# A new order for the 610 steps of the first part of an attention, MLP and mixer kernel

## The chip, the cores and the metric

The kernel runs on one core of a Trainium2 chip. The metric is the device time of one execution in microseconds (us), as the median of the runs. A program's five engines that matter here are TensorE (PE in the profile, with PEld for its weight loads), VectorE (DVE), ScalarE (ACT), GpSimd (POOL) and SyncE (SP, which issues nearly all DMAs).

## What is computed

Three layers in a row, cut to their cores. The first is an attention of 2 batches, 8 heads, 768 positions and head size 64 over a local window and 24 block summaries; the second a layer norm with an MLP of width 2048; the third a mixer over tokens and channels.

```python
# attention
k_sum = k.reshape(B, H, nb, block, D).max(axis=3)
v_sum = v.reshape(B, H, nb, block, D).mean(axis=3)
scores = concat([where(abs(i - j) < 16, scale * q @ k.T, -1e9), scale * q @ k_sum.T + log(block)])
a = softmax(scores);  x = a @ concat([v, v_sum])
# MLP
x = x + relu(layer_norm(x) * g @ w_ch1) @ w_ch2
# mixer
theta = x @ w_theta
u = x + w_tok_r @ (x * cos(theta)) + w_tok_i @ (x * sin(theta))
out = u + relu(u @ w_ch)
```

## The kernel before

The 1536 rows (2 batches of 768) are 12 tiles of 128 rows; tile t has two units, 2t and 2t+1, of four heads each. The MLP works on three chunks of four tiles and goes over 16 slices of its width. The first part of the program, up to the middle of the second chunk, is written as a string of words, `START`. Each word is one step: letters for the kind, a number for the tile, unit, chunk row or weight block. `run` reads the string and issues each step's instructions when its word comes. Every engine runs its instructions in the order in which they were issued, so the string sets the order on each engine, and nothing reorders it afterwards. The words of the steps are:

- DMA loads, issued on SP: `k` keys (0 to 3 of batch 0, 4 to 7 of batch 1), `q` queries (q0 and q1 on ACT's queue), `v` values, `b` values for the block means, `l` a weight block, `M` masks, `J` identity, `G` the norm's gain; `F` with a number not divisible by 3 copies the block means' rows from one value buffer to another.
- attention: `K` block maxima of the keys (DVE), `u` block sums (POOL), `Z` turns them (PE), `F0`, `F3` copy them (ACT); `S` scores of a tile (PE), `m` row maxima (DVE), `N` and `e` bias and exponentials of a unit (ACT), `T` its transposes (PE), `p` or `d` their copy out of PSUM (DVE or ACT), `V` times the values (PE), `R` and `o` the division (DVE).
- layer norm: `n`, `s`, `c` (DVE), `P` (POOL), `dg` (ACT), `fl` (PE), `fh` (ACT), `fz` (DVE) for chunk 0; `h`, `y`, `t` (ACT, DVE, DMA) for chunk 1.
- weights: `A` (ACT), `D` (DVE), `H` (ACT) or `HV` (DVE), `I` (POOL) or `IV` (DVE) turn block l into two float16 halves.
- MLP: `U` up (PE), `i` (ACT), `j` (DVE), `X` down (PE), `Y` adds a result to its tile (DVE).

Buffers are rings that hand out what was given back first: 8 PSUM banks (an `S` takes two, a `T`, `V`, `fl`, `U` one each; `e`, `p` or `d`, `o`, `fz`, `j` give them back), 3 query buffers (q3 overwrites q0's after S0), 3 value buffers, 4 raw buffers for `b` and `l`, 3 buffers for exponentials. The first 12 units' `T` and `V` and the first 8 units' `S` have a dummy matmul (`fill`, from the tile `idle`) ahead of them, and 16 more stand at the very start. Only the words' order is touched by the change; `SECOND` and all later parts, whose order a planner (`Plan`) makes, stay.

Of the kernel before, what the change touches and what calls it, by code (L numbers as in the profile page):

```python
# [14 lines left out]
U16 = mybir.dt.uint16  # L15
# [16 lines left out]
CH = 3 * P  # L32
MC = 4 * P
START = """
q1 J0 q0 M0 k3 k0 k1 k2 b0 b3 b2 b1 q2 v0 v1 v2 K3 K0 K1 K2 G0 S0 u2 k7 k5 S1 m0 k4 k6 m1 N0 u3 e0 l3 S2 m2 q4 N1 e1 q3
m3 N2 u0 b4 e2 T1 m4 q5 T0 m5 d1 T2 N4 p0 e4 u1 b7 p2 N5 T4 N3 e3 e5 T3 b6 K7 Z0 T5 F0 K5 V0 F2 K4 F1 V1 d3 R0 o0 K6 d4
v3 R1 o1 A3 n0 S4 D3 HV3 b5 IV3 S3 q7 m8 m9 N8 e8 s0 c0 S5 u7 q6 N9 m6 e9 m7 V4 N7 m10 q8 e7 V3 m11 u6 l0 N6 R4 V2 o4
N10 d5 R3 o3 T8 N11 R2 v4 o2 V5 n1 e6 u5 T7 l7 s1 c1 v5 d8 T6 d7 R5 o5 T9 d6 n2 V7 e10 s2 u4 l2 V6 R7 e11 o7 T10 R6 v6
o6 S7 n3 d10 P0 l6 s3 A0 d9 Z1 D0 P3 V8 dg0 m15 l1 F3 V9 P1 q10 R8 o8 fl0 HV0 P2 T11 F4 dg1 IV0 v7 fh0 S6 R9 o9 d11 c2
N15 fz0 dg2 fl1 q9 m12 e15 V10 c3 fl2 R10 T15 dg3 o10 m14 V11 fh1 p15 fh2 fl3 F5 fz1 N12 v8 fh3 R11 S8 o11 e12 fz2 fz3  # L40
A2 T12 m13 q11 A6 U0 D2 N13 e13 D6 l5 H2 p12 l10 H6 m16 T13 i0 V12 IV2 I6 N16 V15 e16 j0 U1 R12 o12 N14 R15 e14 o15 p13
A1 m17 V13 n5 i1 T16 D1 N17 v9 e17 T14 S9 R13 l8 o13 H1 s5 j1 A5 I1 p14 T17 A7 m19 V14 P5 D5 N19 e19 D7 l4 H5 X0 R14
l13 o14 H7 I5 m18 v10 A10 IV7 N18 e18 D10 X1 A8 p17 l14 HV10 D8 I10 HV8 A4 T18 l12 p16 I8 V17 d18 D4 V16 V18 A13 R17
l21 o17 T19 H4 R16 v11 o16 R18 d19 I4 S10 o18 D13 HV13 l9 U2 n4 I13 A14 m21 m20 N21 e21 D14 U3 i2 s4 l20 HV14 N20 c4
I14 e20 j2 A21 n7 P4 U4 i3 s7 D21 A12 P7 j3 l23 H21 D12 h4 I21 X2 i4 HV12 l15 c7 A9 I12 j4 h7 D9 U5 A20 HV9 l11 D20 I9
HV20 A23 l18 y7 U6 I20 i5 D23 t7 A15 j5 l17 H23 D15 U7 I23 y4 l22 A11 HV15 t4 c5 I15 T21 D11 A18 V19 p21 X3 l16 D18
HV18 l19 R19 I18 o19 HV11 X4 n9 i6 I11 h5 s9 c9 P9 j6 A17 V21 y5 i7 T20 R21 X5 t5 o21 d20 j7 A22 D17 D22 H17 l27 X6
HV22 l28 n6 I22 h9 s6 c6 I17 X7 y9 A16 P6 n8 D16 A19 V20 HV16 l30 s8 S11 I16 D19 R20 H19 l26 o20 U8 n10 I19 m22 h6 m23
P8 N22 e22 s10 c10 U9 P10 i8 y6 N23 e23 j8 t6 c8 A28 U10 i9 D28 A30 j9 l29 H28 D30 A27 T23 IV28 U11 l24 d23 D27 i10
HV30 H27 l31 j10 A26 IV30 X8 D26 h10 IV27 H26 l25 y10 A29 X9 IV26 i11 D29 j11 H29 A24 T22 IV29 V23 d22 D24 X10 A31 R23  # L50
o23 H24 D31 A25 IV24 H31 X11 D25 IV31 H25 IV25 U12 U13 i12 j12 U14 i13 j13 U15 i14 j14 X12 t10 t9 X13 i15 j15 X14 h8
X15 y8 t8 U16 Y3 Y1 Y0 Y2 U17 i16 j16 X16 i17 j17 X17 U18 U19 i18 j18 X18 i19 j19 X19 U20 U21 i20 j20 X20 i21 j21 U22
X21 i22 j22 X22 V22 U23 R22 o22 n11
"""
SECOND = """
s11 c11 P11 U24 i23 h11 j23 y11 X23 t11 i24 j24 X24 U25 U26 i25 j25 X25 i26 U27 j26 X26 i27 U28 j27 U29 i28 j28 X27 i29
# [1093 lines left out]
```

## Time and profile before

| what | before |
|---|---|
| median of 3 runs | 479.9 us (479.78 to 479.94) |
| the profiled execution: its time | 483.72 us |
| its span, first to last instruction | 481.9 us |
| PE busy | 466.6 us (97%) |
| DVE, ACT, POOL busy | 310.5, 223.0, 229.9 us |
| mean granted PE clock | 0.992 |

A busy PE counts a matmul from its start to a modelled end, and neighbours overlap; a wait that is shorter than that overlap does not show as idle. What a step takes on PE is therefore read from the distance between the starts of two steps, and the number of instructions in a stretch from the counts in brackets.

### The profile page before, as it was taken

The numbers are of one execution on the slowest core, as the hardware profiler recorded it, in microseconds if no ns is written. First come the engines' busy times: TensorE is split into PE (matmuls) and PEld (weight loads), VectorE is DVE, ScalarE is ACT, GpSimd is POOL, SyncE is SP. The second block draws the span as 40 slices with busy tenths as digits, with TensorE's granted clock in tenths as the row PEclk, the third lists the DMA queues.
The fourth block names the chain that finished last, engine by engine and source line by source line (L and its number), as shares of the span: only waits on it lengthen the run. The fifth ranks groups of instructions, "written<-read, shape, count | busy, mean of one in ns | idle before, by whom it ended". The sixth has DMA issues, their size and how long they took to land. (4 is left out here: it accounts for less than half of the span.)

```text
span 481.9 us, 8629 instructions
## 1 busy us (share of the span) xinstructions
PE 466.6 (97%) x3360; PEld 245.9 (51%) x3360; DVE 310.5 (64%) x480; ACT 223.0 (46%) x469; POOL 229.9 (48%) x254
## 2 busy tenths in 40 slices
PE   8888999999999999999999999999998999999997
PEld 3556765445444444444444444444454554566664
DVE  4485899999961311258199898667749588942332
ACT  1564897744851110167176677545525246511122
POOL 3735115655300000049087868556698954792200
PEclk9997999999999999999999999999999999999999
DMA  8996858795681200067287853100076100010012
GB/s 285 307 315 205 264 180 259 253 226 192 203 251 29 43 0 0 1 172 200 65 224 224 238 177 95 39 1 1 0 186 196 23 0 18 33 51 18 0 50 98
DMA packets 44105, 61.71 MB, mean 128 GB/s; under 512 B 23478, under 2 KB 30528, under 8 KB 43680
## 3 DMA queue, kind: packets, MB, share of 16 engines
q1 hardware_dynamic: 43776, 60.63, 43.3%
q8 instruction: 26, 0.43, 0.4%
q10 hardware_dynamic: 288, 0.52, 0.4%
q14 instruction: 15, 0.12, 0.1%
HBM read 48.81 MB, written 6.68 MB: 115 GB/s over the span
## 5 line engine op out<-in xcount | busy, mean ns | idle before, releaser
L111 PEld LDWEIGHTS <-pc 128*128 128x128 f16 x996 | 96.8, 98 | 83.0 <-DMA tok_t<-spilled_t 2.5
L111 PE MATMUL ps<-pc,h 128*128 128x512 f16 x300 | 67.8, 379 | 0.0
L111 PE MATMUL ps<-xt,pc 128*128 128x512 f16 x288 | 65.3, 379 | 0.0
L108 PE MATMUL ps<-xt,pc 128*128 128x512 f16 x288 | 64.2, 379 | 0.0
L108 PE MATMUL ps<-pc,h 128*128 128x512 f16 x276 | 61.4, 379 | 0.0
L111 PE MATMUL ps<-tok_t,pc 128*128 128x384 f16 x288 | 48.8, 326 | 1.7 <-DMA tok_t<-spilled_t 1.7
L111 PEld LDWEIGHTS <-h 128*128 128x128 f16 x300 | 29.3, 98 | 35.4
L108 POOL TENSOR_TENSOR pc<-w,pc 128x512 f16<-128x512 f32 x20 | 27.1, 1361 | 37.6 <-ACT pc L108 22.4
L108 PEld LDWEIGHTS <-pc 128*128 128x128 f16 x288 | 27.8, 98 | 32.8
L108 PEld LDWEIGHTS <-h 128*128 128x128 f16 x276 | 26.8, 98 | 31.8
L108 DVE SCALAR_TENSOR_TENSOR h<-ps,h 128x512 f16<-128x512 f32 x23 | 15.8, 687 | 38.6 <-ACT h L108 38.4
L108 ACT ACTIVATE h<-ps 128x512 f16<-128x512 f32 x23 | 13.8, 600 | 53.8 <-PE ps L108 53.7
L111 PE MATMUL ps<-tok_b,pc 128*128 128x384 f16 x216 | 37.2, 326 | 0.1
L111 POOL TENSOR_TENSOR ve<-mv,eps 128x1 f32<-128x1 f32 x1 | 0.2, 193 | 77.6 <-DVE mv L111 77.6
L111 PE MATMUL ps<-x,pc 128*128 128x384 f16 (+1 forms) x204 | 32.2, 317 | 1.2 <-DVE x L111 1.2
L111 PE MATMUL ps<-th,x 128*128 128x512 f16 x144 | 33.0, 379 | 0.0
L111 DVE SCALAR_TENSOR_TENSOR h<-ps,h 128x512 f16<-128x512 f32 x25 | 17.1, 684 | 21.1 <-ACT h L111 21.1
L111 POOL TENSOR_TENSOR pc<-tr,pc 128x512 f16<-128x512 f32 (+1 forms) x18 | 19.0, 1060 | 20.7 <-ACT pc L111 20.7
L108 ACT ACTIVATE pr<-ps,nb 128x120 f32<-128x120 f32 x96 | 26.6, 365 | 3.9 <-PE ps L108 3.3
L108 POOL TENSOR_TENSOR raw<-raw 128x384 f32<-128x384 f32 (+3 forms) x32 | 18.6, 580 | 17.5 <-DMA raw<-in_vt 15.6
L111 DVE SCALAR_TENSOR_TENSOR w<-raw,hd 128x384 int32<-128x384 int32 (+1 forms) x23 | 22.5, 991 | 6.7 <-ACT hd L111 2.7
L108 DVE SCALAR_TENSOR_TENSOR w<-raw,hd 128x512 int32<-128x512 int32 x32 | 25.2, 795 | 1.1 <-ACT hd L108 1.0
(133 smaller groups left out, 785.9 us busy)
## 6 DMA issues: line engine op xcount, KB each, us to landing
raw<-in_w SPq DMA_DIRECT2D x32, 511.8 KB, 4.6
vw<-in_vp SPq DMA_DIRECT2D x12, 396.0 KB, 6.2
raw<-in_wtr SPq DMA_DIRECT2D x12, 383.8 KB, 4.1
raw<-in_wti SPq DMA_DIRECT2D x12, 383.8 KB, 3.8
k<-in_kw SPq DMA_DIRECT2D x8, 400.0 KB, 8.4
raw<-in_vt SPq DMA_DIRECT2D x8, 384.0 KB, 7.9
qt<-in_qd SPq DMA_DIRECT2D x10, 256.0 KB, 5.3
tok_t<-spilled_t SPq DMA_DIRECT2D x2, 1152.0 KB, 5.8
```

The source lines that it names most:

```text
L108: return getattr(getattr(self.nc, name), method)(*args, **kwargs)
L111: op = Op(len(self.ops), self.ENGINES[name], lambda: getattr(getattr(self.nc, name), method)(*args, **kwargs))
```

## The change

The string `START` holds the same 610 words in another order; no word is added or taken away, and nothing else in the kernel changes. On every engine the same instructions run, in other places. Two pairs of lines of the table:

```diff
-q1 J0 q0 M0 k3 k0 k1 k2 b0 b3 b2 b1 q2 v0 v1 v2 K3 K0 K1 K2 G0 S0 u2 k7 k5 S1 m0 k4 k6 m1 N0 u3 e0 l3 S2 m2 q4 N1 e1 q3
...
+q0 M0 k0 K0 k1 b2 k3 K1 k2 b1 K3 q2 K2 S0 S2 m1 u2 m0 b0 q1 N1 m5 u1 u0 b3 e1 S1 J0 m2 v2 N0 m4 e0 T0 T1 N5 e5 d1 m3
...
```

PE's steps up to the first `U` were

S0 S1 S2 T1 T0 T2 T4 T3 Z0 T5 V0 V1 S4 S3 S5 V4 V3 V2 T8 V5 T7 T6 T9 V7 V6 T10 S7 Z1 V8 V9 fl0 T11 S6 fl1 V10 fl2 T15 V11 fl3 S8 T12 U0

and are now

S0 S2 S1 T0 T1 T5 S3 Z0 T2 T4 V1 V0 S5 V5 T3 T6 V2 V3 V4 S4 T10 T7 V6 T11 S6 S8 V7 T8 T9 S7 V10 T13 fl1 V11 fl2 T12 V8 S9 fl0 V9 Z1 T17 T15 T16 V13 fl3 V12 S10 U0

On SP, the first loads of the program; k0 is the key tile of batch 0 and k1 that of batch 1, raw0 to raw3 hold block values (in_vt) or weights (in_w1, in_w2), qt0 to qt2 queries, vw0 to vw2 values. Before:

```order
L108 DMA ident_181<-in_ident 128x128
L108 DMA mask_l_179<-in_mask_l 69x384
L108 DMA mask_r_180<-in_mask_r 69x480
L108 DMA k0_185<-in_kw 128x800 x4
L108 DMA raw0_160<-in_vt 128x768
...
L108 DMA qt2_184<-in_qd 128x512
L108 DMA vw0_190<-in_vp 96x1056
...
L108 DMA g_sb_74<-in_g_ln 128x512
L108 DMA k1_186<-in_kw 128x800 x4
L108 DMA raw2_162<-in_w2 128x2047
L108 DMA qt1_183<-in_qd 128x512
```

And now:

```order
L108 DMA k0_185<-in_kw 128x800 x2
L108 DMA raw0_160<-in_vt 128x768
L108 DMA k0_185<-in_kw 128x800 x2
L108 DMA raw1_161<-in_vt 128x768
L108 DMA qt2_184<-in_qd 128x512
...
L108 DMA vw2_192<-in_vp 96x1056
L108 DMA qt0_182<-in_qd 128x512
L108 DMA vw0_190<-in_vp 96x1056
...
L108 DMA vw2_192<-vw0_190 24x1056
L108 DMA vw1_191<-vw0_190 24x1056
L108 DMA k1_186<-in_kw 128x800 x3
```

A block load now stands between the second and the third key load of batch 0, the load of q3 (into qt0, which S0 reads) stands ahead of two of the three value loads, and the keys of batch 1 come behind the two copies that wait for `F0`.

On DVE, the place of the first two block maxima of batch 1 (kmax1). Before:

```order
L108 COPY pt1_211<-ps3_66 120x512
L108 COPY pt2_212<-ps1_64 120x512
L108 TENSOR_REDUCE kmax1_188<-k1_186 128x24 x3
L108 RECIPROCAL sums0_203<-ps6_69 128x4
L108 TENSOR_TENSOR x_0_0_75<-ps6_69,sums0_203 128x4x64
L108 TENSOR_REDUCE kmax1_188<-k1_186 128x24
```

And now:

```order
L108 SCALAR_TENSOR_TENSOR w0_164<-raw1_161,hd1_168 128x512
L108 RECIPROCAL sums2_205<-ps4_67 128x4
L108 TENSOR_REDUCE kmax1_188<-k1_186 128x24 x2
L108 TENSOR_TENSOR x_0_2_77<-ps4_67,sums2_205 128x4x64
L108 SCALAR_TENSOR_TENSOR w1_165<-raw0_160,hd0_167 128x512
```

The first maxima of batch 1 stood behind the copies of the first transposes (p0, p2) and ahead of the first result; now two of them stand behind the fifth of R's steps, between `R5` and `o5`, and `o5` gives back a bank that `S4` takes.

## Rows read from the trace of the kernel before

**Rows 1.** Stretches: busy us (instructions) of PE, PEld, DVE, ACT, POOL, clock, DMA share, GB/s.

```profile
0.00:20.40 20.40, 16.17 (x223) 7.90 (x223) 7.85 (x15) 5.03 (x16) 10.40 (x27) 1.00 0.92 281
20.40:37.42 17.02, 13.42 (x255) 9.33 (x255) 12.71 (x22) 11.02 (x37) 9.08 (x18) 0.98 1.01 326
37.42:43.50 6.08, 6.07 (x74) 4.18 (x75) 2.62 (x7) 0.90 (x3) 5.30 (x13) 0.50 0.53 147
43.50:62.50 19.00, 19.00 (x375) 14.67 (x374) 15.93 (x36) 15.75 (x40) 3.02 (x9) 0.99 0.81 238
62.50:143.30 80.80, 79.67 (x704) 42.15 (x703) 74.90 (x129) 54.57 (x120) 33.98 (x34) 1.00 0.78 228
```

**Rows 2.** Timeline of PE: start, length, operation, [idle before, what ended it].

```profile
8.85 0.40 PE L108 MATMUL ps<-k,qt 64*64 64x96 f32 x8 [0.86 <-DMA k<-in_kw]
9.75 0.31 PE L108 MATMUL ps<-kmax,qt 64*64 64x24 f32 x8 [0.50 <-DVE kmax L108]
...
20.48 0.29 PE L108 MATMUL ps<-k,qt 64*64 64x96 f32 x1 [1.97 <-issue]
...
23.76 0.38 PE L108 MATMUL ps<-idle 128*128 128x512 bf16 x1
...
25.09 0.67 PE L108 MATMUL ps<-ident,vpad 128*120 128x128 f32 x4
...
37.43 0.31 PE L108 MATMUL ps<-kmax,qt 64*64 64x24 f32 x3 [3.35 <-issue]
```

**Rows 3.** Timeline of PE: starts of steps without a wait, and of U0.

```profile
14.12 0.39 PE L108 MATMUL ps<-idle 128*128 128x512 bf16 x1
...
16.32 0.39 PE L108 MATMUL ps<-idle 128*128 128x512 bf16 x1
...
49.49 0.57 PE L108 MATMUL ps<-mask_r,mask_l 69*128 69x480 bf16 x2
...
51.24 0.65 PE L108 MATMUL ps<-ident,vpad 128*120 128x128 f32 x4
...
58.40 0.60 PE L108 MATMUL ps<-ident,pr 128*120 128x128 f32 x4
58.84 0.38 PE L108 MATMUL ps<-idle 128*128 128x512 bf16 x1
...
62.52 2.75 PE L108 MATMUL ps<-xt,pc 128*128 128x512 f16 x12
```

**Rows 4.** Timeline of PE: the waits behind U0.

```profile
81.26 1.15 PE L108 MATMUL ps<-vw,pt 121*64 121x65 f32 x32 [0.95 <-DVE pt L108]
...
83.54 0.36 PE L108 MATMUL ps<-mask_r,mask_l 69*128 69x480 bf16 x1 [0.19 <-DVE x L108]
```

**Rows 5.** The page: PE's share and instructions, queue 8, issues to landing.

```profile
PE 466.6 (97%) x3360; PEld 245.9 (51%) x3360; DVE 310.5 (64%) x480; ACT 223.0 (46%) x469; POOL 229.9 (48%) x254
...
q8 instruction: 26, 0.43, 0.4%
...
vw<-in_vp SPq DMA_DIRECT2D x12, 396.0 KB, 6.2
...
k<-in_kw SPq DMA_DIRECT2D x8, 400.0 KB, 8.4
```

**Rows 6.** Timeline of ACT: the first exponentials, and F0.

```profile
14.95 0.21 ACT L108 ACTIVATE nb<-nm 128x4 f32<-128x4 f32 x1 [12.03 <-DVE nm L108]
...
16.18 0.22 ACT L108 ACTIVATE nb<-nm 128x4 f32<-128x4 f32 x1
...
25.91 1.08 ACT L108 ACTIVATE vw<-ps 24x512 f32<-24x512 f32 x2
```

**Rows 7.** DVE by line and form over the first 200 us: mean ns of one.

```profile
L108 DVE SCALAR_TENSOR_TENSOR w<-raw,hd 128x512 int32<-128x512 int32 x32 | 25.2, 795 | 1.1 <-ACT hd L108 1.0
...
L108 DVE TENSOR_REDUCE nm<-ps 128x4 f32<-128x480 f32 x24 | 14.9, 650 | 10.7 <-PE ps L108 10.7
...
L108 DVE TENSOR_REDUCE kmax<-k 128x24 f32<-128x768 f32 x8 | 7.4, 948 | 5.3 <-DMA k<-in_kw 5.2
...
L108 DVE COPY pt<-ps 120x512 f32<-120x512 f32 x9 | 6.1, 683 | 0.3 <-PE ps L108 0.3
```

More of the change, by code (lines that the diff above doesn't have):

```diff
@@ L34 @@
 START = """
-q1 J0 q0 M0 k3 k0 k1 k2 b0 b3 b2 b1 q2 v0 v1 v2 K3 K0 K1 K2 G0 S0 u2 k7 k5 S1 m0 k4 k6 m1 N0 u3 e0 l3 S2 m2 q4 N1 e1 q3
[L36 to L53, printed above, removed]
+q0 M0 k0 K0 k1 b2 k3 K1 k2 b1 K3 q2 K2 S0 S2 m1 u2 m0 b0 q1 N1 m5 u1 u0 b3 e1 S1 J0 m2 v2 N0 m4 e0 T0 T1 N5 e5 d1 m3
@@ new lines @@
+u3 N4 T5 N2 q3 e4 e2 S3 Z0 T2 d5 v0 m7 q5 F0 N3 p0 T4 v1 e3 m6 V1 N6 V0 p2 q4 l6 R1 R0 l9 d4 F2 F1 S5 o0 k5 o1 A6 n0
+V5 T3 m10 m11 s0 e6 A9 k7 N10 T6 d3 V2 D9 k4 R5 K5 K7 l7 N11 o5 V3 D6 e11 e10 v3 q6 V4 S4 R4 N7 o4 d6 n2 m8 R3 e7 T10
+T7 d10 o3 H6 A7 d7 m9 N8 R2 K4 s2 k6 b4 P0 K6 N9 V6 P2 q8 G0 o2 T11 n1 u4 S6 D7 e8 s1 R6 e9 m12 q7 H7 m13 b5 S8 V7 c1
+q9 d11 m16 N12 v5 IV7 N13 T8 m17 e12 N16 o6 T9 S7 e13 P1 R7 o7 n3 c2 dg1 m15 m14 s3 V10 T13 e16 b7 d8 p13 fl1 R10 dg2
+V11 o10 fl2 R11 N17 N15 v4 N14 e17 c0 d9 fh2 T12 b6 o11 u5 fh1 u7 c3 v6 V8 fz2 l0 fz1 R8 u6 S9 dg0 o8 fl0 P3 V9 q10
@@ new lines @@
+m19 p12 R9 e15 fh0 fz0 o9 l8 l2 N19 A0 Z1 D0 T17 T15 T16 F3 V13 l4 dg3 fl3 p15 p17 F5 q11 e19 fh3 HV9 F4 I9 A2 HV0 V12
+fz3 R13 IV0 S10 D2 e14 o13 H2 l10 IV2 A4 v8 A8 U0 D4 m18 U1 H4 R12 m21 o12 N18 I4 T14 p16 v7 m20 l3 i0 e18 n4 I6 U2 j0
+N21 A10 V15 D10 l1 i1 j1 V17 N20 T18 e21 T19 R15 l5 HV10 o15 I10 A3 p14 V16 d18 V14 U5 T21 i2 R17 D3 v9 R16 D8 e20 n6
+HV8 A1 d19 D1 l20 R14 I8 o16 j2 o17 T20 HV3 S11 l12 A20 o14 m23 n8 H1 A5 m22 IV3 V19 D5 D20 d20 HV20 H5 R19 I1 o19 N23
+V18 U3 l22 n7 v10 e23 U4 I5 l13 p21 A12 N22 D12 R18 o18 A22 I20 s4 n5 e22 c4 X0 l11 X1 D22 i3 A13 HV22 A11 j3 I22 D11
@@ new lines @@
+l16 V21 T22 HV12 v11 R21 i4 A16 l30 o21 s5 I12 d22 s8 X2 D16 T23 HV11 I11 HV16 j4 D13 V22 V20 d23 s7 l14 A14 V23 R20
+R22 X3 o20 R23 o22 U6 o23 D14 X4 I16 n9 HV13 A30 l18 s9 U8 l24 l15 HV14 A18 P4 i5 i6 j5 D30 I14 D18 A15 j6 l19 i8 HV18
+P9 I18 I13 l17 X5 c5 P5 n10 h5 HV30 D15 A19 D19 X6 l21 U9 IV30 h4 H19 y5 A24 c7 l26 D24 l25 s6 y4 HV15 I15 I19 A26 A17
+U7 i7 D26 t4 j8 D17 i9 j7 H26 l27 s10 A21 l31 H17 IV26 H24 U10 X7 P6 A25 c6 D25 l23 P7 h7 A31 H25 I17 D21 l28 IV24 U11
+X8 H21 U13 A23 i11 D23 H23 i10 l29 A28 j9 P8 y7 I23 D31 I21 A29 U12 t5 H31 IV25 h6 D28 j10 X9 y6 D29 t6 i12 H29 U15 t7
@@ L54 @@
+X10 P10 c9 j11 H28 j12 X11 U18 IV28 i15 h9 U17 i13 A27 c8 D27 IV31 H27 IV29 j13 IV27 y9 j15 c10 X12 U14 i14 X13 h10
+U16 i17 j14 U19 j17 y10 X14 X15 Y2 i19 j19 U20 U23 Y0 Y3 i16 j16 X16 i18 X17 n11 t9 j18 h8 i20 X18 Y1 U21 X19 i21 y8
+t8 j21 j20 X20 U22 i22 j22 X21 t10 X22
 """
```

## The prediction

> **What bounds the kernel now.** The first thing to read is the table of stretches [rows 1]. PE is busy in all of 43.5 to 62.5 us and of 79.67 of the next 80.80 us, and the page has it at 97% of the span [rows 5]. The end of the program is thus set by PE's own work plus the moments in which it stands still. The word table keeps every instruction, so PE's work is the same and only its stops can change. Nearly all of them lie ahead of 43.5 us: PE is busy 16.17 of 20.40 us, then 13.42 of 17.02, then the whole of 6.08 us, but at a granted clock of 0.50 [rows 1].
>
> The timeline of PE names them [rows 2]. Scores of tile 0 wait 0.86 for a key load and 0.50 for the block maxima. Two stops are put down to "issue", 1.97 and 3.35 us: PE waited for no other engine. Queue 8 brought 26 packets of instructions, and PE runs 3360 + 3360 of them [rows 5]: one packet for 258. Ahead of the first stop lie 223 + 223 instructions, between the two 255 + 255 [rows 1], two packets' worth. So I read both stops as PE waiting for its next block of instructions, and a block can be late after every 258 or so. The second stop was followed by 6.08 us at half clock, the first by none: 3.04 us lost. And T4 took 1.33 us from its dummy at 23.76 to Z0 at 25.09, some 0.7 more than a transpose's 0.44 [rows 3] and its dummy. Sum ahead of U0 at 62.52: 0.86 + 0.50 + 1.97 + 3.35 + 3.04 + 0.7 = 10.4 us. Behind U0 the flagged waits are 0.95 + 0.19 = 1.1 [rows 4]. About 11.5 us is the most that any order of the first part could give.
>
> **The change, on PE.** Ahead of U0 the new order puts two more S (1.75 each, 49.49 to 51.24), three more T (0.44 each, 58.40 to 58.84) [rows 3] and two more V (1.15 for a pair [rows 4]): 3.5 + 1.3 + 1.15 = 6.0 us that stood later. The old order with that work would have U0 at 62.52 + 6.0 = 68.5; the new one without any stop has it at 68.5 - 10.4 = 58.1. What matters is which stops come instead. I walked along the new order with these step times.
>
> (a) Scores of tile 0. k0 is now the first key load, and identity and k3 no longer stand ahead of it, so the first head pair waits less than the 0.86 + 0.50. But a block load stands ahead of the third key load, so k2 lands about when it did, and its maximum is DVE's fourth at 0.95 [rows 7]: the third head pair waits. Bounds 0.3 (only the handover) and 1.4 (as before); I take 0.8.
>
> (b) The stop in the third S. The instruction counts up to there are the same, so block 2 ends in the same place, near the end of S1 instead of S2. But SP now holds q3 back until S0 has read its buffer, and behind q3 stand v0, q5 and v1: where the old order had DMAs queued without a break (share 0.92 and 1.01 [rows 1]), the queue runs nearly dry when the block is asked for. Bounds 0 and 1.97; I take 0.4, near the dry queue.
>
> (c) Around F0. V1 needs F0 (1.08 on ACT [rows 6]) right behind Z0. The two copies F2 and F1 wait on SP for F0, and k5, k7, k4 stand behind them; K5 and K7 on DVE wait for those, and o5, which frees a bank for S4, stands behind K7. In between, PE has S5, V5, T3, T6, V2, V3, V4, about 8 us. A key load took 8.4 us to land [rows 5], but from a full queue; here SP has just waited, so I take half of that, and then two maxima at 0.95 just fit. Bounds 0 and 3; I take 0.6.
>
> (d) S6 needs the maximum K6. On DVE that stands behind m8 and m9, which need S4's end: two at 0.65, two K at 0.95 [rows 7] and about 1 us of short steps, 4.2 us; PE has T10, T7, V6, T11 and half of S6 to do, about 3.8. Wait 0.4 (0 to 1). In the same way S7's second bank comes from o6, behind m16 and m17: about 2.4 us from S8's end against 2.2 of V7, T8, T9; 0.5 with the handover (0 to 1.5).
>
> (e) The block that ends in S8. S6 and S8 are neighbours, 264 instructions in 3.5 us, the densest place of the new order, and by count a block begins with S6 and ends with S8. From 43.5 to 62.5 some 750 instructions, three blocks, came without a stop in 19 us, 6.3 us for each, at a DMA share of 0.81; the late one was not there at 34.1 us, though the instructions of one block ahead of it, two S, take about 4 us, and came 3.35 us later, so its fetch took some 7.4. If the fetch takes 4 to 5 us in a half-filled queue, the stop is 0.5 to 1.5. Bounds 0 and 3.0 + 3.0 for a clock that falls; I take 0.8.
>
> [...]
>
> (f) DVE and ACT. Ahead of U0 DVE now has three more D (0.795), m (0.65) and p (0.68) [rows 7] and about 1.3 us of IV, R and o: 7.7 us. ACT has five more N and e at 1.23 (14.95 to 16.18 [rows 6]), 6.2, and six weight steps. From 20.4 to 62.5 DVE idled 42.1 - 12.71 - 2.62 - 15.93 = 10.8 us and ACT 14.4 [rows 1], so DVE is the tighter one. For what it makes PE wait beyond (c) and (d) I take 1.0 (0 to 7, third rival).
>
> Sum of new stops ahead of U0: 0.8 + 0.4 + 0.6 + 0.4 + 0.5 + 0.8 + 1.0 = 4.5; U0 at 58.1 + 4.5 = 62.6, so 5.9 us earlier for the same work. Behind U0 DVE stays the tight one until about the tenth U (it was busy 74.90 of 80.80 us there [rows 1]); I take 2.1 us of waits instead of 1.1. Everything later is PE bound and unchanged, since its order and its work are. Gain 5.9 - 1.0 = 4.9 us. The profiled execution (483.72 us, span 481.9) would come to 478.8; its 3.8 us over the median I take as the profile's own, so 479.9 - 4.9 = 475.0.
>
> **The rivals.**
> 1. Little of it stays (chance 0.12). DVE, brought forward by 7.7 us, must also bring forward what X0 and its neighbours need, and at 93% busy behind U0 it can give back only part: PE waits 3 us more there. 478.0.
> 2. The stops stay (0.10): the fetch of the S6 and S8 block takes as long as the late one did, 7.4 us against 3.5, and the clock falls: 6.0 instead of 0.8. Gain 4.9 - 5.2 = -0.3: 480.2, no change. For it: the old stop also came among neighbouring S's. Against it: SP waits for S6's query buffer just then. [...]
> 3. Slower (0.12): DVE's gaps stay. From 20.4 to U0 at 62.6 it may idle only 42.2 - 31.3 - 7.7 = 3.2 us. The gaps came from results of PE and from loads (a maximum behind a late key blocks all behind it), and the new order has K5 and K7 in just such a place. If DVE idles the 10.8 us that it did, U0 comes 7.6 us later, 70.2 against 68.5, and the time is 479.9 - 4.9 + 7.6 = 482.6. It decides from 8.1 us of idle time on.
>
> **How the numbers follow.** The forecast, 475.0, has 0.60; its own range, from the lower ends of (a) to (f) to most of their sizes doubled, is 471 to 478. A better case with nearly no stop (1.5 us in all and none behind U0, gain 10) is 470.0 and has 0.06. Then 0.12 for 478.0, 0.10 for 480.2, 0.12 for 482.6. Leaving out the last two, and nothing below, the range is 470.0 to 479.3. A measurement of this kernel tells 0.2%, about 1 us, from no change. Faster by over that: 0.60 + 0.06 + 0.12 = 0.78; within it: 0.09, most of the second rival; slower: 0.13.
>
> **What would show it.** Right: on PE no issue stop over 1.5 us, a granted clock of 1.00 from 20 to 62 us, U0 near 62 us, DVE idle under 4 us between 20 and 62. (b) would be wrong if the stop near 18 us still has 2 us; (c) if S4 or V5 waits for DVE or a DMA for over 1 us; (e) if a stop over 2 us comes near 42 us; (f) if PE waits for DVE or ACT by over 2 us ahead of U0. The whole is wrong if PE's stops ahead of the first U still add up to 10 us, or if new ones over 3 us come behind it.

## The result, and the profile after

| what | before | after |
|---|---|---|
| median of the runs taken side by side | 479.92 us (479.78 to 482.75) | 475.15 us (474.69 to 476.16) |
| ratio, with 95% interval | | 0.989 (0.9849 to 0.993) |
| the profiled execution: time, span | 483.72, 481.9 us | 476.16, 474.4 us |
| start of U0 | 62.52 us | 63.72 us, with 6.0 us more work ahead of it |
| from U0 to the 24th U | 141.11 us | 132.47 us, with 6.0 us less work in it |

The kernel became 1.1% faster, 4.8 us by the medians, where 475.0 had been forecast. From the 24th U on the two traces run alike (278.3 and 278.2 us to the end), so all of the difference lies in front of it.

The stretches of after, cut at the same times and with the same columns as [rows 1]:

```profile
0.00:20.40 20.40, 17.50 (x248) 9.58 (x249) 9.07 (x17) 5.44 (x17) 14.29 (x35) 1.00 0.92 279
20.40:37.42 17.02, 16.10 (x339) 11.70 (x336) 12.69 (x27) 14.47 (x48) 1.32 (x3) 1.00 0.94 277
37.42:43.50 6.08, 4.84 (x148) 3.76 (x149) 4.54 (x11) 4.28 (x18) 3.65 (x7) 1.00 0.91 318
43.50:62.50 19.00, 17.99 (x310) 13.87 (x309) 15.60 (x34) 14.61 (x43) 11.30 (x21) 0.91 0.85 240
62.50:143.30 80.80, 80.80 (x638) 41.76 (x638) 62.17 (x118) 45.92 (x94) 32.80 (x34) 1.00 0.73 223
```

PE, the third column, has few gaps up to 43.5 us and none behind 62.5; its clock is 1.00 except in the fourth stretch. DVE, the fifth, is at 62.17 us in the last stretch where it was at 74.90 [rows 1].

The timeline of PE in after, with all its waits up to the second layer, answers [rows 2]:

```profile
0.98 5.39 PE L108 MATMUL ps<-idle 128*128 128x512 bf16 x17 [0.98 <-DVE idle L108]
...
7.43 0.40 PE L108 MATMUL ps<-k,qt 64*64 64x96 f32 x8 [0.43 <-DMA k<-in_kw]
8.33 0.31 PE L108 MATMUL ps<-kmax,qt 64*64 64x24 f32 x8 [0.50 <-DVE kmax L108]
...
11.39 0.40 PE L108 MATMUL ps<-k,qt 64*64 64x96 f32 x8 [0.41 <-DMA k<-in_kw]
12.38 0.31 PE L108 MATMUL ps<-kmax,qt 64*64 64x24 f32 x8 [0.59 <-DVE kmax L108]
...
14.00 0.39 PE L108 MATMUL ps<-idle 128*128 128x512 bf16 x1
...
37.84 0.69 PE L108 MATMUL ps<-vw,pt 121*64 121x65 f32 x16 [1.34 <-DMA vw<-in_vp]
...
44.51 0.30 PE L108 MATMUL ps<-kmax,qt 64*64 64x24 f32 x5 [1.83 <-issue]
```

The stop of [rows 2] near 20 us is gone, and so is the one at 37 us. Two new ones stand in their place: V6 waits 1.34 us for a value load, and S8 stops 1.83 us with five matmuls to go. Right behind that stop the clock falls, as a cut of that stretch shows (columns as above):

```profile
45.06:48.47 3.41, 3.41 (x27) 2.82 (x27) 3.34 (x8) 1.64 (x6) 2.70 (x4) 0.51 1.03 266
```

The granted clock stands at 1.00 or at 0.50 in these two traces, and at the lower one here (0.51 over the cut); 3.41 us of it cost PE about 1.7 us of work, by estimate from that clock.

The 24th U, the first matmuls of line L111, in before and in after:

```profile
203.63 1.24 PE L111 MATMUL ps<-xt,pc 128*128 128x512 f16 x5
```

```profile
196.19 2.75 PE L111 MATMUL ps<-xt,pc 128*128 128x512 f16 x12
```

### The profile page after: what moved, and what is told of

Its sections match the earlier page's. It is cut to its first block, busy times and chain, and to the rows that moved or that the text cites. A ratio compares the mean times of both kernels' runs of the same rounds, so it can differ in the third digit from the quotient of the medians.

```text
span 474.4 us, 8632 instructions
## 1 busy us (share of the span) xinstructions
PE 462.2 (97%) x3360; PEld 244.8 (52%) x3360; DVE 302.4 (64%) x480; ACT 220.8 (47%) x469; POOL 231.6 (49%) x254
## 5 line engine op out<-in xcount | busy, mean ns | idle before, releaser
L111 PEld LDWEIGHTS <-pc 128*128 128x128 f16 x996 | 96.8, 98 | 82.9 <-DMA tok_t<-spilled_t 2.0
L111 PE MATMUL ps<-pc,h 128*128 128x512 f16 x300 | 67.8, 379 | 0.0
L111 PE MATMUL ps<-xt,pc 128*128 128x512 f16 x288 | 65.3, 379 | 0.0
L111 PE MATMUL ps<-tok_t,pc 128*128 128x384 f16 x288 | 48.8, 326 | 1.2 <-DMA tok_t<-spilled_t 1.2
L111 PEld LDWEIGHTS <-h 128*128 128x128 f16 x300 | 29.4, 98 | 35.4
L108 POOL TENSOR_TENSOR pc<-w,pc 128x512 f16<-128x512 f32 x20 | 25.3, 1277 | 42.3 <-DVE pc L108 26.5
L111 PE MATMUL ps<-tok_b,pc 128*128 128x384 f16 x216 | 37.2, 326 | 0.0
L108 ACT ACTIVATE h<-ps 128x512 f16<-128x512 f32 x23 | 13.5, 593 | 50.9 <-PE ps L108 50.9
L111 DVE SCALAR_TENSOR_TENSOR h<-ps,h 128x512 f16<-128x512 f32 x25 | 17.1, 685 | 30.7 <-ACT h L111 30.7
L108 DVE SCALAR_TENSOR_TENSOR w<-raw,hd 128x512 int32<-128x512 int32 x32 | 26.3, 830 | 14.9 <-ACT hd L108 10.1
L111 PE MATMUL ps<-x,pc 128*128 128x384 f16 (+1 forms) x204 | 32.4, 317 | 1.4 <-DVE x L111 1.3
L111 PE MATMUL ps<-th,x 128*128 128x512 f16 x144 | 33.0, 379 | 0.0
L111 POOL TENSOR_TENSOR pc<-tr,pc 128x512 f16<-128x512 f32 (+1 forms) x18 | 19.2, 1075 | 20.7 <-ACT pc L111 20.7
L108 ACT ACTIVATE hd<-raw 128x512 f16<-128x512 bf16 x32 | 24.5, 785 | 10.0 <-DMA raw<-in_w 4.7
L111 DVE SCALAR_TENSOR_TENSOR w<-raw,hd 128x384 int32<-128x384 int32 (+1 forms) x23 | 22.5, 991 | 7.3 <-POOL xt L111 3.3
L111 ACT ACTIVATE h<-ps 128x512 f16<-128x512 f32 x25 | 14.7, 586 | 22.9 <-PE ps L111 18.5
```

The source lines that it names most:

```text
L108: return getattr(getattr(self.nc, name), method)(*args, **kwargs)
L111: op = Op(len(self.ops), self.ENGINES[name], lambda: getattr(getattr(self.nc, name), method)(*args, **kwargs))
```

## The experiments

U0 and the distance from U0 to the 24th U are read from each run's timeline of PE, the time at half clock from its granted clock in steps of half a microsecond, up to U0; in the first two traces that time is 6.8 us for before and 3.4 for after. A ratio stands against the kernel before on the same chip, whose medians there were 480.13, 480.49, 480.48 and 480.55 us. The diffs below show only the piece of the table that differs.

| run | median us | ratio (95%) | U0 | U0 to 24th U | half clock ahead of U0 |
|---|---|---|---|---|---|
| before again | 480.48 | 1.001 (0.9989 to 1.003) | 58.60 | 141.12 | 3.4 |
| new head, old rest | 478.88 | 0.9981 (0.9957 to 1.0005) | 58.95 | 141.12 | 10.2 |
| old head, new rest | 482.48 | 1.0032 (1.0005 to 1.0058) | 70.75 | 133.13 | 6.8 |
| before, S's spread | 481.11 | 1.0018 (0.9995 to 1.0041) | 60.44 | 141.12 | 3.4 |
| before, two copies on ACT | 479.25 | 0.9972 (0.995 to 0.9995) | 60.56 | 139.81 | 3.4 |
| before, cut dummies | 480.53 | 1.0001 (0.9974 to 1.0028) | 59.09 | 141.12 | 3.4 |
| the same, b2 early | 480.04 | 0.9995 (0.9972 to 1.0019) | 58.29 | 141.12 | 0 |
| after, cut dummies | 475.68 | 0.9894 (0.9876 to 0.9913) | 63.72 | 132.48 | 3.4 |
| after, full queue | 478.24 | 0.9956 (0.9939 to 0.9974) | 65.81 | 132.48 | 3.4 |
| after, v3 early | 474.95 | 0.9884 (0.9864 to 0.9903) | 62.23 | 132.47 | 0 |
| after again | 476.13 | 0.9894 (0.9837 to 0.9951) | 63.62 | 132.48 | 3.4 |
| after, v3 early, again | 474.59 | 0.9859 (0.9792 to 0.9927) | 62.58 | 132.48 | 0 |

The last column is the steadiest number of the study: 141.12 for every old rest but the one with copies on ACT, 132.48 for every new one but that behind the old head. The column of U0 isn't as clean: the clock falls at another place and for another time in each trace, and about half of that time is lost, by estimate from a clock of 0.50.

**The kernel before, once more, unchanged.**

> The kernel before, unchanged, to see how much of the first profile's two stops and half clock belongs to every execution. Theory (PE's late instruction blocks): a stop of 1.5 to 2.5 us near 18.5 us and one of 3 to 4 us near 34 us come again, behind the same instruction counts (about 446, and 510 more); the ratio to the kernel before is 1.00. Rival (the stops are chance of one execution): they come in other places or not at all. Open: whether the half clock behind the second stop comes every time; the first profiled execution was 3.8 us above the median, about what it costs (3.04 us), so I expect it in some executions only.

The timeline of PE, its two stops:

```profile
20.70 0.29 PE L108 MATMUL ps<-k,qt 64*64 64x96 f32 x1 [1.99 <-issue]
...
36.16 0.25 PE L108 MATMUL ps<-kmax,qt 64*64 64x24 f32 x3 [1.34 <-issue]
```

Both stand at the very instructions of [rows 2], with one matmul and three to go; so their place belongs to the program. The size of the second doesn't: 1.34 here, 3.35 in the first trace. Nor does the place of the half clock: it is 1.00 behind the second stop here, from 37.42 to 62.5 us, and falls behind the first, where the first trace had none (columns as in [rows 1]):

```profile
21.96:25.37 3.41, 3.41 (x16) 2.82 (x15) 2.19 (x4) 3.34 (x14) 2.94 (x8) 0.50 1.04 405
```

U0 comes at 58.60, 3.9 us sooner: 2.0 from the smaller stop and about 1.7 from 3.4 us of half clock instead of 6.8. Together that is nearly all of the 3.8 us by which the first profiled execution lay above its median.

**The new order up to T2, then the old order's rest.**

```diff
-T2 d5 v0 m7 q5 F0 N3 p0 T4
+T2 v0 v1 G0 k7 k5 k4 k6 l3 q4 b4 q5 p0 b7 p2 T4
```

> The new order's words up to T2 (its loads, S0, S2, S1, the first transposes and S3), then the old order's words that are left. S4 and S5 are neighbours again, behind V0 and V1. Theory (late blocks): no stop near 18 us, since SP holds q3 back; but the block that ends in S5 is dense again (V1, S4 and most of S5, about 4 us), so a stop of 2.5 to 4 us near 32 to 34 us stays. Time 1 to 3 us below before, 477 to 479. Rival (the gain is the first loads' order): all of it, about 4.8 us, 475.

Timeline of PE, the one wait behind tile 0:

```profile
29.73 0.60 PE L108 MATMUL ps<-k,qt 64*64 64x96 f32 x8 [2.31 <-DMA qt<-in_qd]
```

No stop came near 18 us nor where one had been expected later; scores waited 2.31 us for their queries instead, since the old rest loads two value tiles, four key tiles and a weight block ahead of them. The head alone saves nothing that can be told from 0. Part of what it saves may be lost again to the clock: it is 0.50 from 29.02 to 39.26 us, beginning in that wait, the longest such stretch of all traces.

**The old order up to T2, then the new order's rest.**

```diff
-T2 N4 p0 e4 u1 b7 p2 N5 T4
+T2 u1 N5 e5 N4 T5 e4 S3 Z0 d5 m7 F0 N3 p0 T4
```

> The mirror: the old order's words up to T2, then the new order's words that are left. Theory (late blocks): the stop near 18.5 us stays at about 2 us, since v0, v1, v2 and more stand in the queue when the block is asked for; no stop near 34 us, since S5 is spread from S3 and S4; the one of about 1.8 us in S8 stays. Time 2 to 4 us below before, 476 to 478. Rival (the first loads' order): no gain, 479.5 to 480.5.

```profile
21.34 0.29 PE L108 MATMUL ps<-k,qt 64*64 64x96 f32 x1 [1.85 <-issue]
...
30.62 0.60 PE L108 MATMUL ps<-k,qt 64*64 64x96 f32 x8 [5.00 <-DMA qt<-in_qd]
```

The stop of the old head stayed, as expected, and the forecast of a gain was wrong: in the old head q3 stands behind four key tiles, a weight block and q4, and S3, which the new rest runs early, waits 5.00 us for it. But 133.13 us from U0 on, the gain behind U0 is there although the head is the old one. The two halves of the order thus aren't separable in front of U0, and the gain behind U0 belongs to the rest alone.

**Three neighbouring S's of the old order drawn apart.**

```diff
-S5 u7 q6 N9 m6 e9 m7 V4 N7 m10 q8 e7 V3 m11 u6 l0 N6 R4 V2 o4
+u7 q6 N9 m6 e9 m7 V4 N7 e7 V3 u6 l0 N6 R4 V2 S5 m10 m11 q8 o4
```

> The old order with four words moved: S5 with its m10, m11 and q8 goes from behind S3 to behind V2, so that V4, V3 and V2 stand between the second and the third of the three neighbouring scores. Theory (late blocks): the block that was late is then asked for as early as before but wanted about 1.3 us later (V4, V3 and part of V2 in place of part of S5), so the stop near 34 us shrinks from 3.35 to about 2 us, and with under 2 us no half clock follows it (none followed the stop of 1.97 us): 1 to 4 us below before. Rival (the stop is not tied to the instruction count): 3.35 us as before, no gain.

```profile
37.82 0.36 PE L108 MATMUL ps<-mask_r,mask_l 69*128 69x480 bf16 x1 [0.85 <-ACT pr L108]
41.17 0.38 PE L108 MATMUL ps<-idle 128*128 128x512 bf16 x1 [0.81 <-DVE x L108]
51.63 0.55 PE L108 MATMUL ps<-ident,xn 128*128 128x128 f32 x3 [0.60 <-issue]
```

The stop near 36 us went; 0.85 and 0.81 us of waits for PSUM banks and a new small stop came, and a stretch at half clock behind the waits of tile 0 (10.69 to 14.11). Taking a stop away by hand gained nothing.

**The 16 first dummies cut in four, in the changed kernel and in the one before.** Both get 48 matmuls and 48 weight loads more at the very start, so every block of instructions ends 48 matmuls earlier in the order.

```diff
     for i in range(16):
-        fill(warm)
+        for r in range(4):
+            nc.tensor.matmul(warm[:, r * P:(r + 1) * P], idle, idle, start=True, stop=True)
```

> The changed kernel with each of the 16 dummy matmuls of 512 columns at the very start cut into four of 128: the same columns, 96 instructions more ahead of S0, so every block of PE's instructions ends 96 instructions earlier in the program. The block that ended in S8's last matmuls then ends a quarter into S8, and holds V6, T11 and T10 besides; the next one ends in S7. The dummies may end about 1 us later, which S0's wait for the third key load hides. Theory (late blocks): the stop of 1.83 us in S8 goes; one of at most 1 us may come in S7; V6 still waits 1.3 us for its values. U0 1 to 2 us earlier against the changed kernel's 63.7, or 2 to 4 if no half clock comes; time 472 to 474.5 against 475.15. Rival (the stop belongs to the place, for instance to S8 and the loads of that moment, not to the count): the stop stays in S8, 475 to 476.

Timeline of PE, the only stop for instructions that is left:

```profile
54.76 0.25 PE L108 MATMUL ps<-kmax,qt 64*64 64x24 f32 x4 [2.15 <-issue]
```

S8's stop is gone, S9 has one. It has 988 matmuls ahead of it, where S8's has 732 ahead (both counted along the timeline): two blocks of 128. The place is an instruction count. What one stop gave, the other took back: 475.68 us, where 472 to 474.5 had been expected.

> The kernel before, with each of the 16 dummy matmuls at the very start cut in four of 128 columns (48 matmuls and 48 weight loads more, so that every block of instructions ends 48 matmuls earlier in the order). Theory (a stop stands where a block of instructions ends, so its place is an instruction count): in the kernel before the first stop had 223 matmuls ahead of it and the last but one matmul pair of the third S behind it; with 48 more ahead, again 223 matmuls stand ahead of the stop, and its place is the first head pair of the third S, near 17.5 us. Its size stays 1.5 to 2.8 us since the DMA queue is full there in this order. The second stop, then 478 matmuls from the start, moves from the last head of its S to the S before or the first head pairs, 0.5 to 1.5 us earlier. Time 478 to 482, the same as before within 0.5%. Rival (the stops belong to a step, a bank or a load, not to a count): both stay at the step where they were, with 271 matmuls ahead of the first.

PE's wait, and the chain of block sums on POOL (first and last of four):

```profile
25.50 0.54 PE L108 MATMUL ps<-ident,vpad 128*120 128x128 f32 x3 [2.23 <-POOL vpad L108]
```

```profile
14.40 2.49 POOL L108 TENSOR_TENSOR raw<-raw 128x384 f32<-128x384 f32 x4 [9.07 <-DMA raw<-in_vt]
...
25.21 0.23 POOL L108 TENSOR_TENSOR vpad<-raw 128x24 f32<-128x24 f32 x1
```

Neither early stop came, not even at the new border near 17.5 us, where one had been expected. And still nothing was gained: Z0 had to wait 2.23 us for POOL, whose sums begin when the first block load lands and take 2.7 us each. In the kernel before the stop had hidden that.

**The same, with the first block load ahead of two key loads.**

```diff
-k3 k0 k1 k2 b0 b3 b2 b1
+k3 k0 b2 k1 k2 b0 b3 b1
```

> The kernel before with the 16 dummies cut in four, as in the run before, and with the first block load (b2) ahead of the last two key loads of batch 0 on SP. With the cut dummies alone the two early stops were gone and the time was the same: Z0 waited 2.23 us for the fourth block sum of POOL (at 25.50), whose chain of four sums of 2.7 us began at 14.40 with the landing of the first block load. Theory (POOL's chain, set by the place of the block loads, is the next bound of the old order, and the stop near 18 us only hid it): b2 lands 2 to 4 us sooner, the chain ends at 21.5 to 23.5, Z0's wait is under 0.5, and tile 0's scores wait 0.5 to 1.5 us longer for the last keys; U0 at 57.5 to 58.5 instead of 59.09, time 478.5 to 480. Rival (PE is held elsewhere by then, by a stop that comes back or by the later key loads): Z0's wait is gone but U0 stays at 59.1 or later, time 480 to 482.

POOL's last sum, and PE's waits behind it:

```profile
22.96 0.23 POOL L108 TENSOR_TENSOR vpad<-raw 128x24 f32<-128x24 f32 x1
```

```profile
29.09 0.40 PE L108 MATMUL ps<-k,qt 64*64 64x96 f32 x8 [1.11 <-DMA qt<-in_qd]
...
35.81 0.69 PE L108 MATMUL ps<-vw,pt 121*64 121x65 f32 x16 [1.11 <-DMA vw<-vw]
```

The chain ends 2.25 us sooner and Z0's wait is gone, as expected; U0 is only 0.8 us sooner, because S's queries and the copied means' rows, 1.11 us each, are late next. Even that 0.8 isn't the edit's alone, since the run with cut dummies had 3.4 us at half clock and this one none. Two limits were peeled off the old order by hand, and the time is that of before within its interval.

**Two value loads ahead of q3 in the changed kernel**, to fill the DMA queue when block 2 is asked for.

```diff
-q3 e4 e2 S3 Z0 T2 d5 v0 m7 q5 F0 N3 p0 T4 v1 e3 m6
+v0 v1 q3 e4 e2 S3 Z0 T2 d5 m7 q5 F0 N3 p0 T4 e3 m6
```

> The changed kernel with two loads moved on SP: v0 and v1 go ahead of q3, so they are issued at once and do not wait for S0. The DMA queue is then full when PE asks for the block that it enters near 14 us, as in the kernel before. Theory (a queued load delays the block): a stop of 1.5 to 2.2 us near 18 us in S1, where the changed kernel has none; q3 lands about 4 us later, at 21 to 22, and S3 may wait up to 1 us more; 476 to 478. Rival (the first block's fetch does not depend on what is queued): no stop near 18, 475 to 476.

PE, then SP's issues (start, length, count) in this run, and SP's in the changed kernel:

```profile
21.00 0.29 PE L108 MATMUL ps<-k,qt 64*64 64x96 f32 x1 [2.50 <-issue]
```

```profile
14.27 7.46 SPq L108 DMA_DIRECT2D qt<-in_qd  x3
```

```profile
14.15 0.33 SPq L108 DMA_DIRECT2D qt<-in_qd  x1
14.53 0.43 SPq L108 DMA_DIRECT2D vw<-in_vp  x1
16.35 0.33 SPq L108 DMA_DIRECT2D qt<-in_qd  x1
```

With two transfers more in the queue the stop is back at the instruction where the old order had it, 2.50 us long, and the median is 3.1 us above the 475.15 of after (0.9956 of before instead of 0.989). SP took 7.46 us over three query loads here and 0.33 over each of them there.

**v3's load ahead of a weight load in the changed kernel.**

```diff
-K5 K7 l7 N11 o5 V3 D6 e11 e10 v3 q6
+K5 K7 v3 l7 N11 o5 V3 D6 e11 e10 q6
```

> The changed kernel with one load moved on SP: v3 goes ahead of l7. V6 waited 1.34 us for v3; ahead of the 512 KB of l7 it should land some 1.7 us sooner. Theory (that wait is on PE's path): V6 does not wait, and what follows up to S8 comes 1.3 us sooner; the stop in S8 may grow by part of it, since the block that begins with S6 is asked for sooner into a queue that is as full. Time 0.3 to 1.3 us below the changed kernel, 473.8 to 474.9. Rival (the stop takes all of it): the stop in S8 grows to about 3 us, 475.2. l7 lands 2 us later; if A7 waits for it on ACT, d7 and V7 come later by up to 1 us.

```profile
43.40 0.30 PE L108 MATMUL ps<-kmax,qt 64*64 64x24 f32 x5 [1.12 <-issue]
...
46.79 0.36 PE L108 MATMUL ps<-mask_r,mask_l 69*128 69x480 bf16 x1 [0.54 <-DVE x L108]
```

V6's wait of 1.34 is gone, S8's stop is at its old place, and S7 now waits 0.54 for the bank that o6 gives back. To see how much of it is the edit's, it ran again beside the changed kernel:

> The changed kernel, unchanged, beside the version with v3 loaded early on the same chip. Theory: 475.2 (474.5 to 476.2); no stop near 18 us, a wait of 1.0 to 1.5 for v3's load ahead of V6 and a stop of 1.5 to 2.0 in S8 near 42 to 45 us at the same instruction counts as in its first profile. Rival (these two were that execution's own): one of them is under 0.5 us or stands elsewhere.

```profile
37.53 0.69 PE L108 MATMUL ps<-vw,pt 121*64 121x65 f32 x16 [0.96 <-DMA vw<-in_vp]
...
44.41 0.30 PE L108 MATMUL ps<-kmax,qt 64*64 64x24 f32 x5 [2.03 <-issue]
```

> The changed kernel with v3's load ahead of the weight block l7 on SP, once more. Theory (it saves the wait for v3, of which the first profile showed 1.34 in the changed kernel and none here): 0.3 to 1.3 us faster than the changed kernel in the same call, 474.0 to 475.0, with U0 near 62.2. Rival (what is saved there comes back as a longer stop in S8 or as waits of S7 for its bank): the same as the changed kernel within 0.3 us.

```profile
43.43 0.30 PE L108 MATMUL ps<-kmax,qt 64*64 64x24 f32 x5 [0.27 <-issue]
```

The two waits of after are its program's own, and the version with v3 early beats it by 1.5 us side by side: 474.03 to 475.03 against 475.34 to 476.63. It is the fastest kernel of the study. Part of that is the clock: both traces with v3 early keep 1.00 up to U0, and all four executions beside after show a granted clock of 1.000, of after's own only one of four, that of 475.34 us. Against that one the four are 0.8 us faster on average; whether the edit also keeps the clock up isn't shown.

**Two copies of transposes on ACT instead of DVE, in the kernel before.**

```diff
-p17
+d17
...
-p16
+d16
```

> The kernel before with the copies of units 16 and 17 out of PSUM moved from DVE to ACT (p16, p17 become d16, d17). In the kernel before V16 waited 0.95 us near 80 us for DVE's copy, which stood behind three slower steps, while ACT waited 2.0 us for a load. Theory (behind U0 the kernel before loses about 2.2 us because DVE is late, and the new order does not): that wait goes or moves to ACT, and the time from U0 to U24 falls by 0.5 to 1.2 us from 141.1; 479 to 480 against 480.1. Rival (the time behind U0 is PE's own): the wait goes, and U24 comes no sooner because S10 waits for a bank instead; no change.

The wait of 0.95 us behind U0 [rows 4] is gone, and U0 to the 24th U falls by 1.3 us, from 141.12 to 139.81: the one old tail that differs. So a late copy on DVE was part of what before lost behind U0.

## Why the prediction was right, and where it wasn't

The total was right, and partly by luck. Ahead of U0 5.9 us were forecast and 0.9 measured against an ordinary execution of before; behind U0 a loss of 1.0 was forecast and 2.6 were won. The two errors nearly cancelled. Of the four signs by which the prediction wanted to be known as right, only U0 came near (63.72 for 62): a stop of 1.83 us is over its 1.5, the clock fell, and DVE idled 9.3 us instead of under 4.

**(a) Tile 0** was taken at 0.8 us and measured 0.43 + 0.50 + 0.41 + 0.59 = 1.93, above the upper bound of 1.4. The third head pair did wait, as walked; the first wasn't spared as much as assumed. Part of it is only apparent: the dummies took 5.39 us, 1.0 less than the 6.39 in the trace of before, so PE came to the same landing sooner. The second S began at 14.00, where it had begun at 14.12 [rows 3].

**(b) The first stop** was put at 0.4 for a nearly dry queue; it was 0. The reason was tried by filling the queue, and 2.50 us came back at that instruction. The queue wasn't dry, though: the DMA share was 0.98 from 14.0 to 18.3 us. What SP had issued by then made the difference. But the gain booked for it was too large. A stop of 1.97 was taken as lost time, and 0.7 at T4 as a small extra. The cut dummies showed that Z0, right behind T4, was the real limit: without the stop Z0 waits 2.23 for POOL. The changed order has that too, in an edit that the prediction didn't cost, the earlier block loads. POOL's chain of sums in before, and in after:

```profile
14.11 2.49 POOL L108 TENSOR_TENSOR raw<-raw 128x384 f32<-128x384 f32 x4 [8.79 <-DMA raw<-in_vt]
...
24.93 0.23 POOL L108 TENSOR_TENSOR vpad<-raw 128x24 f32<-128x24 f32 x1
```

```profile
9.47 2.47 POOL L108 TENSOR_TENSOR raw<-raw 128x384 f32<-128x384 f32 x4 [4.15 <-DMA raw<-in_vt]
...
20.45 0.22 POOL L108 TENSOR_TENSOR vpad<-raw 128x24 f32<-128x24 f32 x1
```

It ends at 25.16 in before, just when Z0 starts (25.09, [rows 2]), and 4.5 us sooner in after, where nobody waits for it.

**(c) F0's surroundings** (0.6) and **(d) S6 and S7** (0.9) measured 0. Bound by bound they were possible: S7 waits for o6 by 0.17 to 0.54 in the runs with v3 early and with cut dummies. What stood in between instead was not seen, the load of v3: 1.34 us at V6.

**(e) The block that ends in S8** came exactly where the instruction count put it, but with 1.83 us and a clock of 0.51 behind it for 3.41 us, together 3.5 instead of 0.8. That the clock would hold was the wrong part, and the stop itself was twice the 0.8. The second rival's 6.0 wasn't reached.

That the order has a hold on the stops is shown: two of the 26 blocks of before cost PE a stop, 1.97 and 3.35 us, at fixed counts; S8's went and S9 got one, two blocks on, when 48 matmuls were put ahead; and the first one, absent in after, came back with 2.50 us when two loads were put into the queue.

**(f) DVE and ACT ahead of U0** were given 1.0, with a third rival by which DVE's idle time had to fall to 3.2 us. Measured: DVE idled 42.1 - 12.69 - 4.54 - 15.60 = 9.3 us from 20.4 to 62.5, and PE didn't wait for it once in that time. The rival's condition (over 8.1 us) was met and its effect didn't come. The count of steps was right: when PE came to U0 at 63.72, DVE had run all that stand ahead of it but two, which come next, o13 and IV2:

```profile
63.66 0.68 DVE L108 SCALAR_TENSOR_TENSOR w<-raw,hd 128x512 int32<-128x512 int32 x1
64.26 0.41 DVE L108 TENSOR_TENSOR x<-ps,sums 128x256 f32<-128x256 f32 x1
65.02 0.69 DVE L108 TENSOR_TENSOR pc<-w,pc 128x512 f16<-128x512 f32 x1 [0.35 <-ACT pc L108]
```

What failed was their price: DVE was busy 43.1 us up to U0, 4.0 more than before up to its U0 (39.1), and with the two 5.1 instead of 7.7. A step's length was added up, but the next one starts before it ends (0.60 us behind the first of these lines, which is 0.68 long), and D took 0.68 instead of the 0.795 of all [rows 7]; the rest of the 2.6 stays open. Besides, 1.2 us of the work was done ahead of 20.4 us (9.07 against 7.85), and U0 stood 1.1 us later than forecast, both of which the rival's 3.2 us left out.

**Sum ahead of U0.** 1.93 + 1.34 + 1.83 + 1.7 = 6.8 less the 1.0 of the dummies is 5.8, on 58.1: 63.9, and U0 stands at 63.72 (62.6 forecast). Against the profiled execution that is 68.5 - 63.7 = 4.8 us of gain. Against an ordinary one it is much less: with U0 at 58.60, as in the second trace of before, 58.6 + 6.0 - 63.7 = 0.9. The prediction called the 3.8 us by which its profile lay over the median "the profile's own" and left them out of the end time, but had counted the same 3.35 us stop and its 3.04 us of clock into the gain. That was a double use of one number. The medians differ by 4.8, more than the 3.5 of the two profiles below, because the profiled execution of after lay 1.0 us above its own median. Where the granted clock was 0.999 or more, the spans were 477.5 us in 12 of the 81 executions of before beside the experiments and 473.4 in 3 of the 8 of after, on average: 4.1 us with the clock left out.

**Behind U0** 1.0 us was to be lost; 141.11 - 6.0 - 132.47 = 2.6 were won, in every pair of runs. With the 0.9 ahead of U0 that makes 3.5, the difference of the spans of the second trace of before (477.9) and of after (474.4). The flagged waits [rows 4] are 1.1 of the 2.6, and the copies on ACT gave 1.3. Where the first of them came from, the rows of DVE and POOL in the kernel before show:

```profile
78.29 0.41 DVE L108 CAST pc<-w 128x512 f16<-128x512 f32 x1
...
79.34 1.27 DVE L108 CAST pc<-w 128x512 f16<-128x512 f32 x1
80.53 0.68 DVE L108 COPY pt<-ps 120x512 f32<-120x512 f32 x1
```

```profile
78.79 1.54 POOL L108 TENSOR_TENSOR pc<-w,pc 128x512 f16<-128x512 f32 x1 [2.16 <-DVE pc L108]
```

The same cast took 0.41 us at 78.29 and 1.27 at 79.34, while POOL's step ran from 78.79 to 80.33; it ended 0.28 us after POOL's. The copy behind it ended at 81.21, and V, at 81.26 with 0.95 of waiting, started with it. DVE's casts over the time up to the 24th U, in before and in after (the last numbers ahead of the idle time are their sum and their mean in ns):

```profile
L108 DVE CAST pc<-w 128x512 f16<-128x512 f32 x15 | 9.5, 633 | 0.3
```

```profile
L108 DVE CAST pc<-w 128x512 f16<-128x512 f32 x15 | 6.4, 438 | 0.1
```

Four of before's 15 began while a step of POOL was running, and these are the slow ones; in after it was one. "DVE stays the tight one" was wrong: it is busy 62.17 of 80.80 us, 12.7 less, 3.0 of it by the casts and most of the rest with eleven instructions fewer there (118 for 129).

The other 1.4 us or so of the 2.6 stand in no row as a wait, but they do in the distances between starts. Summed over U0 to the 24th U, a matmul of U takes the same in both traces (216 ns), while one of V takes 42 ns in before and 34 in after, and one of T 130 and 120. A V took longer where it stood alone:

```profile
65.64 1.15 PE L108 MATMUL ps<-vw,pt 121*64 121x65 f32 x32
66.72 2.76 PE L108 MATMUL ps<-xt,pc 128*128 128x512 f16 x12
69.42 0.69 PE L108 MATMUL ps<-vw,pt 121*64 121x65 f32 x16
70.03 1.09 PE L108 MATMUL ps<-ident,pr 128*120 128x128 f32 x8
```

One V alone took 0.61 us (69.42 to 70.03), two in a row 1.08 (65.64 to 66.72). One T took 0.53 ahead of a V (65.11 to 65.64) and 0.44 ahead of a U (128.79 to 129.23). In ten places of before's stretch V starts anew, in five of after's. V's surplus is 1.6 us with the flagged 0.95 in it, T's 0.4, that of the masks with the flagged 0.19 and of X 0.6: together the 2.6, and at after's prices the moved steps come to 6.0 again.

**How long a stop is** can be read from queue 8, an instruction queue of the trace: its 26 packets of 16 KB come to 258 each of PE's 3360 + 3360 instructions [rows 5]. The trace has each packet's start and landing (us):

| run, border of a block | packet starts, lands | PE goes on | behind the landing | stop |
|---|---|---|---|---|
| before, first | 17.68, 18.93 | 20.48 | 1.55 | 1.97 |
| before, second | 34.59, 35.82 | 37.43 | 1.61 | 3.35 |
| before, cut dummies, first | 13.75, 15.11 | 17.58 | 2.47 | none |
| after, first | 14.99, 16.24 | 18.14 | 1.90 | none |
| after, S8 | 42.08, 43.18 | 44.51 | 1.33 | 1.83 |
| after, full queue, first | 18.39, 19.67 | 21.00 | 1.33 | 2.50 |
| after, v3 early, S8 | 40.90, 41.98 | 43.40 | 1.42 | 1.12 |
| the same, again, S8 | 40.90, 41.98 | 43.43 | 1.45 | 0.27 |

All 21 stops of over 0.2 us that the 14 traces put down to "issue" ahead of U0 end 1.2 to 1.6 us behind the landing of such a packet. So they are late instruction blocks, as the prediction had only inferred from counts, and their size is the landing plus some 1.4 us less the time at which PE reaches the border: the last two rows have the same landing, but PE came to the border at 42.28 and at 43.16. Two loads more in the queue moved the first packet from 14.99 to 18.39.

What stays open is when a packet starts: over the first seven borders of the 14 traces that was from 1.1 us before to 6.2 us after PE entered the block ahead of it. Neither the density of a block nor the share of the DMA engines tells it alone: the block in front of the first border was run in 4.3 us in after (14.0 to 18.3) without a stop, at a DMA share of 0.98, and in the kernel before with cut dummies one was run in 3.3 us (30.5 to 33.8) without any, while the 128 matmuls in front of S8's stop took 3.3 us without it in after (5.1 from 39.4 to 44.5).

## What to carry to other kernels

A stop in a tuned timetable hides what is late behind it: before a stop is booked as gain, look for the next limit of the same step (here POOL's sums, then queries, then the copied rows), because taking one away by hand gave 0 three times and only a joint new order of loads and steps gave 1.1%. Take gain and base from the same execution, and look at a second profile of the kernel before when its profiled time is above its median, since the excess may be the very stop that is to be removed. Compare the granted clock of two traces before their starts are compared, since a stretch at half clock moved from trace to trace (it began at 36.89 us in before, at 21.96 in its second trace). And take what a step costs an engine from the distance between starts, on DVE as on PE, and by the steps that stand next to it.

## What was unexpected of the hardware

PE's stops for its own instructions came at fixed instruction counts, about 128 matmuls with their weight loads apart or multiples of it (223 and 478 matmuls ahead of them in before, 732 in after, 988 in after with cut dummies), with sizes from 0.27 to 3.35 us (S8: 1.83 and 2.03, with a full queue 1.58, with v3 early 1.12 and 0.27; the second of before: 3.35, 1.34 and, with two copies on ACT behind it, 2.09). Each ended 1.2 to 1.6 us behind the landing of a 16 KB packet on the instruction queue.

A cast to float16 on DVE took 0.40 to 0.43 us in the 25 places, of the two traces up to the 24th U, where no step of POOL was running when it began, and 0.77 to 1.27 us in the five where one was. In these five it ended 0.28 us behind that step. Why is not shown.
